# Six late output stores moved to another queue, and a score-operand load requested earlier

## The chip, the cores and the metric

The kernel runs on one core of a Trainium2 chip. The metric is the device time of one execution in microseconds (us). A core has five engines that run their own instruction streams and meet only at semaphores: TensorE (PE; its weight loads are listed as PEld), VectorE (DVE), ScalarE (ACT), GpSimd (POOL) and SyncE (SP). In this kernel SP does nothing but issue DMA transfers; POOL computes and also issues some. In the profile a name such as SPq or POOLq is the queue of that engine, where it waits and issues.

## The reference

One input `x` (2048 rows of 576, float32) is normalised; an attention block of 32 heads of 18 columns and a bilinear feed-forward block are both computed from it, and joined:

```
xn = layernorm(x)
s  = (softmax(q k^T * 18**-0.5) v, heads joined) @ wo      # q, k, v = xn @ wqkv
g  = silu(((xn @ w_gate) * (xn @ w_up)) @ w_down)          # inner width 4608
out = x + s * g
```

## The kernel before

Products on TensorE are made from pairs of a high and a low part of each number, so that several narrow matrix products add up to a precise one. The kernel has three stages.

**The opening** (to about 200 us) normalises `x`, makes q, k and v and puts them into DRAM scratch.

**The middle** (to about 2530 us) runs attention and the feed-forward block at once on TensorE. Attention takes the heads h = 0 to 31 in turn. For each head there are two passes over 64 scores (16 row blocks by 4 column blocks): the first pass ("a", L585) makes scores only to take row maxima on DVE (L587), the second ("b", L617) makes the transposed scores, which ACT exponentiates (L619). Then come the products with v (L628). The feed-forward block takes 72 units (4 chunks of 512 rows, 18 groups of 256 inner columns) with gate and up products (L667) and down products (L709).

The score passes read two kinds of stacked operands in SBUF. `pairs` are two tiles that alternate between heads; `ring` is a single tile that all heads use in turn, in two halves of 1024 columns each. `load_ring(r, h, k)` fills half k for head h, in rows 0 on (r = 0, for pass a) or rows 64 on (r = 64, for pass b), with three DMAs on SP's queue (L242). The first half serves the scores 0 to 31 of a pass, the second half 32 to 63. A load may go out when the head before has done its last score with that half.

The order of all this is not written out by hand: `order()` simulates the engines with fixed durations (`clk`, `free`, `banks`, `queue`) and emits instructions as its clock advances. A load that has become possible is put into a list `stacks` by `feed` (called before each score). It leaves the list in one of two ways: at the end of a gate block, where up to two of the listed loads are sent, or at a fixed score of the pass, by the table at L947, if it is still waiting then. `send` issues it and books its bytes on the simulated DMA queue; scores are held until their operands have arrived by that booking.

SP executes its queue strictly in order. Between the ring loads stand loads of gate and up weights (`wgu`, L182, 1152 KB, which wait until TensorE has finished with the buffer), of down weights (`wd`, L217), of the swapped halves of the feed-forward activations (`hx`, L699), of `xc` (L361, L364) and of `vt` (L573).

**The end** (from about 2530 us) multiplies the attention result with `wo`, tile by tile: 16 tiles t of 128 rows, each in two halves of 288 columns (L1218). `give(t, ps, last)` finishes a tile. For each half DVE multiplies the product in PSUM by the gate (L1227); then `x` is added and the tile stored. With `last` false, POOL adds (L1232) and the whole tile of 288 KB is stored by a DMA that POOL issues (L1234). With `last` true, DVE adds (L1229) and each half of 144 KB is stored by SP (L1230). Before the change only tile 15 has `last` true. After `give(t)` the kernel fetches what tile t + 6 needs (`xi`, `gin`; L831, L833), on SP's queue, so that the last fetch stands behind `give(9)`. POOL also does the last step of the gates of tiles 12 to 15 here (L765). L1283 is the end of the program, where every engine drains and all meet.

Of the kernel before, what the change touches and what calls it, by code (L numbers as in the profile page):

```python
# [40 lines left out]
def kernel(  # L41
# [10 lines left out]
    nc = tc.nc  # L52
# [5 lines left out]
    NT = S // 128  # L58
# [31 lines left out]
    out2 = out.rearrange("o s d -> (o s) d")  # L90
# [43 lines left out]
    def chore(all=True):  # L134
        q = (all and chores) or later
        if q:
            f, a = q.pop(0)
            f(*a)
# [5 lines left out]
    def ready(done, key):  # L144
        while key not in done:
            assert chores or later
            chore()
# [419 lines left out]
    with ExitStack() as mid:  # L567
# [240 lines left out]
        def high(k, c):  # L808
            if k == 0:
                hi[c] = fin["ep"].tile([128, 5, 512], FR, name="hi", bufs=2)  # L810
            nc.scalar.activation(hi[c][:, k, :], lo[k][:, 512 * c:512 * c + 512].bitcast(FT), AF.Copy)

        def low(k, c):
            part = lo[k][:, 512 * c:512 * c + 512]
            if k < 4:
                nc.vector.tensor_tensor(part, part.bitcast(FT), hi[c][:, k, :].bitcast(FT), op=OP.subtract)
            else:
                nc.vector.tensor_tensor(hi[c][64:128, 4, :], part[64:128].bitcast(FT), hi[c][64:128, 4, :].bitcast(FT),
                                        op=OP.subtract)
# [6 lines left out]
        def fetch(t):  # L826
            rows = slice(t * 128, (t + 1) * 128)
            if t < 12:
                ready(sdone, t)
                gin[t] = fin["ep"].tile([128, D], FT, name="gin", bufs=7)  # L830
                nc.sync.dma_start(gin[t], sg[rows, :])  # L831
            xi[t] = fin["ep"].tile([128, D], FT, name="xi", bufs=8)
            nc.sync.dma_start(xi[t], x2[rows, :])  # L833
# [94 lines left out]
        def send(want, now):  # L928
            f, a = want
            f(*a)  # L930
            arrives[f.__name__, *a] = moved(now, 0.44 if f is load_pair else 0.22)
# [6 lines left out]
        def feed(r, h, i):  # L938

            if i == 0:  # L940
                if h:
                    stacks.append((load_ring, (r, h, 1)))
                if h + 1 < H and (r or h):
                    stacks.append((load_pair, (r, h + 1)))
            if i == 32 and h + 1 < H:
                stacks.append((load_ring, (r, h + 1, 0)))
            for at, want in ((20, (load_ring, (r, h, 1))), (48, (load_pair, (r, h + 1))), (52, (load_ring, (r, h + 1, 0)))):  # L947
                if i == at and want in stacks:
                    stacks.remove(want)
                    send(want, max(clk))  # L950

        def a_next(r=0):
            nonlocal na
            h, i = divmod(na, N)
            feed(0, h, i)
            a_item(h, i, r)
            slot = turn["a"] % 2
            turn["a"] += 1
            banks["a"][slot] = engine("DVE", issue(r, LONG), 0.60) + EARLY
            na += 1  # L960
            if i == N - 1:
                max_fold(h)
                max_rows(h)
                rows_done[h] = engine("DVE", 0.0, 0.85) + ROWS
# [5 lines left out]
        def b_next(r=1):  # L970
            nonlocal nb
            h, i = divmod(nb, N)
            feed(64, h, i)
            if i == 16 and h % 2 == 0 and h // 2 + 1 < H // 2:
                load_v(h // 2 + 1)
            b_item(h, i, r)
            slot = turn["b"] % 2
            turn["b"] += 1
            end = engine("ACT", issue(r, LONG), 0.495)
            banks["b"][slot] = end + EARLY  # L980
            nb += 1
            if i % 4 == 3:
                due.append((h, i // 4, end + 0.03))
# [222 lines left out]
    def banks_of(t):  # L1206
        return [bank("ab"[t % 4], 2) if t % 4 < 2 else bank("g", 1, 2 * (t % 4) - 4 + h) for h in range(2)]
# [5 lines left out]
    def product(t, h, p, ps):  # L1213
        a, e = p
        c, r = divmod(t, 4)
        w = wov["w"][:, a, :] if a < 8 else wov["w2"][:, a - 8, :]
        o = lo[e - 4][:, t * 128:(t + 1) * 128] if 4 <= e < 8 else hi[c][:, min(e, 4), r * 128:(r + 1) * 128]
        nc.tensor.matmul(ps[h][:, 0:HALF], o, w[:, h * HALF:(h + 1) * HALF], start=p == ALL[0], stop=p == ALL[-1])  # L1218

    def give(t, ps, last=False):  # L1220
        y = ys[:, t % 4, :]
        ready(sdone, t)
        g = gin.pop(t)
        xt = xi.pop(t)
        for h in range(2):
            cs = slice(h * HALF, (h + 1) * HALF)
            nc.vector.tensor_tensor(y[:, cs], ps[h][:, 0:HALF], g[:, cs], op=OP.mult)  # L1227
            if last:
                nc.vector.tensor_tensor(y[:, cs], y[:, cs], xt[:, cs], op=OP.add)  # L1229
                nc.sync.dma_start(out2[t * 128:(t + 1) * 128, cs], y[:, cs])  # L1230
            else:
                nc.gpsimd.tensor_tensor(y[:, cs], y[:, cs], xt[:, cs], op=OP.add)  # L1232
        if not last:
            nc.gpsimd.dma_start(out2[t * 128:(t + 1) * 128, :], y)  # L1234

    ys = wpool.tile([128, 4, D], FT, name="ys", tag="wd", bufs=1)
    ps = {t: banks_of(t) for t in range(4)}
# [6 lines left out]
    for t in range(NT):  # L1244
        if t >= 4:
            ps[t] = banks_of(t)
        for h in range(2):
            for p in ORDER[2] if t < 4 else ALL:
                product(t, h, p, ps[t])
        for _ in range((2, 0, 0, 0, 2, 2, 1, 0, 2, 2, 1, 0, 0, 0, 0, 0)[t]):  # L1250
            if split:
                k, c = split.pop(0)
                high(k, c)
                low(k, c)
        give(t, ps.pop(t), t == NT - 1)
        if t + 6 < NT and t + 6 not in xi:
            fetch(t + 6)
        for _ in range((1, 1, 3, 3)[t % 4] if t < 12 else 4):
            chore()
# [28 lines left out]
```

## Time and profile before

| | us |
|---|---|
| median of 3 runs (2599.17 to 2603.44) | 2601.77 |
| the profiled execution, whole | 2602.83 |
| its span, first to last instruction | 2601.1 |
| TensorE busy in the span | 2576.5 |
| VectorE busy | 1919.9 |
| ScalarE busy | 1462.6 |
| GpSimd busy | 590.7 |

The granted clock of TensorE was 0.998 of full speed. "Busy" counts computing instructions; time in which a queue waits, drains or issues a DMA is listed apart. A row of the waits has the engine that waited, the line and tile, the releaser, and then us in total, times, and the longest. A row of a timeline has start, duration, engine, line, operation, output and inputs, and the count of merged instructions; in brackets stands the idle time before it with what ended it. A row for one source line has count, shortest, median and longest duration in ns, and the first and last start in us.

### The profile page before, as it was taken

How to read it: one execution, taken by the hardware profiler on the slowest of the kernel's cores; microseconds unless marked ns; L12 is line 12 of the kernel's file. 1: busy time of each engine (PE TensorE's matmuls, PEld its weight loads, DVE VectorE, ACT ScalarE, POOL GpSimd, SP SyncE). 2: the span in 40 equal slices, each digit the busy share in tenths (PEclk: the TensorE clock that was granted, in tenths of full speed). 3: DMA queues.
4: the chain of work that ended last, by engine and by line, in shares of the span. 5: the costliest groups of instructions: out<-in, count | busy, mean ns of one | idle time of the engine just before them, and what ended most of it. 6: DMA issues, size and time to landing. Idle time of an engine off the chain costs nothing.

```text
span 2601.1 us, 59086 instructions
## 1 busy us (share of the span) xinstructions
PE 2576.5 (99%) x24360; PEld 2109.3 (81%) x24360; DVE 1919.9 (74%) x3373; ACT 1462.6 (56%) x2698; POOL 590.7 (23%) x658
## 2 busy tenths in 40 slices
PE   8999999999999999999999999999999999999998
PEld 6899877788878788878878878877788888877878
DVE  6208777777768888877788788777788888777537
ACT  5222666666655555655555565555555665555561
POOL 3114444434421111111111112111111211111115
PEclk9999999999999999999999999999999999999999
DMA  7799989888786666565676556656686666665566
GB/s 237 221 283 275 269 226 227 227 217 220 218 190 181 178 180 178 171 182 157 177 195 176 167 172 181 177 164 174 157 202 157 175 184 175 176 174 168 150 187 232
DMA packets 195433, 504.57 MB, mean 194 GB/s; under 512 B 58096, under 2 KB 116080, under 8 KB 156124
## 3 DMA queue, kind: packets, MB, share of 16 engines
q1 hardware_dynamic: 184812, 487.58, 67.1%
q0 software_dynamic: 10352, 13.22, 1.9%
q8 instruction: 192, 3.15, 0.5%
q14 instruction: 77, 0.63, 0.1%
HBM read 312.21 MB, written 107.61 MB: 161 GB/s over the span
## 4 chain that ended last, share of the span: by engine, by line
PE 97%; DVE 1%; DMA 1%; ACT 0%; SPq 0%; issue 0%; ACTq 0%; DVEq 0%
PE pg L667 34%; PE pg L628 17%; PE pg L709 16%; PE pa L585 11%; PE pb L617 9%; PE pg L395 2%; PE pa L341 2%; PE pb L341 2%; PE pg L1218 1%; PE pa L1218 1%; PE pb L1218 1%; DMA ring<-sqk 0%; DMA hx<-hs 0%; ACT xn L289 0%; DMA xin<-in_A_x_dram 0%
## 5 line engine op out<-in xcount | busy, mean ns | idle before, releaser
L587 DVE TENSOR_REDUCE mx<-pa 128x1 f32<-128x512 f32 x2048 | 1361.8, 684 | 159.7 <-PE pa L585 73.3
L619 ACT ACTIVATE pt<-pb 128x512 f32<-128x512 f32 x2048 | 1155.1, 597 | 566.8 <-PE pb L617 484.4
L667 PE MATMUL pg<-xc,wgu 64*128 64x512 f32 x7776 | 1397.5, 392 | 0.3 <-DMA xc<-sx 0.3
L667 PEld LDWEIGHTS pg<-xc,wgu 64*128 64x128 f32 x7776 | 1056.3, 186 | 49.8 <-DMA xc<-sx 0.7
L617 PE MATMUL pb<-pair,ring 56*128 56x512 f32 x2006 | 789.1, 399 | 2.2 <-DMA ring<-sqk 2.2
L585 PE MATMUL pa<-pair,ring 54*128 54x512 f32 x2001 | 784.7, 398 | 0.3 <-DVE mx L587 0.3
L709 PE MATMUL pg<-wd,hs 64*128 64x288 f32 x3408 | 536.6, 292 | 1.2 <-DVE acc L737 1.2
L709 PE MATMUL pg<-wd,hx 64*128 64x288 f32 x3408 | 528.6, 292 | 0.4 <-DMA hx<-hs 0.4
L709 PEld LDWEIGHTS pg<-wd,hs 64*128 64x128 f32 x3408 | 473.4, 186 | 5.8 <-DVE acc L737 1.9
L709 PEld LDWEIGHTS pg<-wd,hx 64*128 64x128 f32 x3408 | 467.8, 185 | 4.4 <-DMA hx<-hs 1.0
L628 PE MATMUL pg<-pt,vt 128*32 128x512 f32 x4096 | 456.5, 596 | 0.0
L683 POOL TENSOR_TENSOR hs<-us,hs 128x512 fp32r<-128x512 f32 x144 | 186.2, 1293 | 1129.5 <-ACT hs L682 1112.9
L585 PEld LDWEIGHTS pa<-pair,ring 54*128 54x128 f32 x2001 | 363.2, 184 | 81.7 <-issue 47.8
L617 PEld LDWEIGHTS pb<-pair,ring 56*128 56x128 f32 x2006 | 364.7, 184 | 14.4 <-issue 3.4
L628 PEld LDWEIGHTS pg<-pt,vt 128*32 128x32 f32 x4096 | 125.9, 110 | 285.8 <-issue 281.9
L634 DVE TENSOR_TENSOR oc<-oc,pg 128x512 f32<-128x512 f32 x69 | 47.4, 687 | 323.5 <-PE pg L628 323.3
L737 DVE TENSOR_TENSOR acc<-acc,pg 128x288 f32<-128x288 f32 x544 | 234.0, 443 | 27.0 <-PE pg L709 24.2
L682 ACT ACTIVATE hs<-us 128x512 fp32r<-128x512 f32 x144 | 91.0, 632 | 154.2 <-DVE us L679 151.6
L648 POOL DMA_DIRECT2D sot<-oc x124 | 64.1, 523 | 332.8 <-DVE oc L645 330.7
L607 POOL DMA_DIRECT2D pair<-mt x128 | 78.0, 615 | 226.0 <-DVE mt L602 223.8
L632 ACT ACTIVATE oc<-pg 128x512 f32<-128x512 f32 x32 | 19.2, 599 | 189.3 <-PE pg L628 189.3
L191 POOL TENSOR_TENSOR wgu<-wraw,wgu 128x384 fp32r<-128x384 f32 x108 | 108.4, 1017 | 75.3 <-ACT wgu L190 70.4
(128 smaller groups left out, 1384.0 us busy)
## 6 DMA issues: line engine op xcount, KB each, us to landing
wgu<-swg SPq DMA_DIRECT2D x102, 1152.0 KB
hx<-hs SPq DMA_DIRECT2D x142, 512.0 KB
wd<-swd SPq DMA_DIRECT2D x50, 1152.0 KB
swg<-wgu SPq DMA_DIRECT2D x36, 1152.0 KB
pair<-sqk SPq DMA_DIRECT2D x192, 144.0 KB
ring<-sqk SPq DMA_DIRECT2D x384, 72.0 KB
swd<-wd SPq DMA_DIRECT2D x18, 1152.0 KB
sqk<-hl SPq DMA_DIRECT2D x32, 512.0 KB
```

The lines of the kernel that those rows point to most:

```text
L191: nc.gpsimd.tensor_tensor(w[:, 9 + b:12 + b, :], raw[:, b:b + 3, :], w[:, b:b + 3, :].bitcast(FT), op=OP.subtract)
L341: nc.tensor.matmul(p, wq[b, a], xcs[c][:, e, :], start=n == 0, stop=n == len(PAIRS) - 1)
L585: nc.tensor.matmul(p, q[rows, t * 128:(t + 1) * 128], k[rows, c * 512:(c + 1) * 512], start=True, stop=True)
L587: nc.vector.tensor_reduce(mx[h][:, t, c:c + 1], p, axis=AX.X, op=OP.max)
L617: nc.tensor.matmul(p, k[rows, t * 128:(t + 1) * 128], q[rows, c * 512:(c + 1) * 512], start=True, stop=True)
L619: nc.scalar.activation(pt[t, c], p, AF.Exp, scale=scale)
L628: nc.tensor.matmul(p[32 * c:32 * c + 32, :], vt[h // 2][:, t, 6 * (h % 2):6 * (h % 2) + 32], pt[t, c], start=t == ts[0], stop=t == ts[-1])
L667: nc.tensor.matmul(ps, gw[n][half[r], a, :], xg[i][half[r], e, :], start=k == 0, stop=k == len(TERMS) - 1)
L682: nc.scalar.activation(hj[:, 0, :], h32, AF.Copy)
L683: nc.gpsimd.tensor_tensor(hj[:, 1, :], h32, hj[:, 0, :].bitcast(FT), op=OP.subtract)
L709: nc.tensor.matmul(ps[:, 0:HALF], (hx if k else hs)[u][half[r], j, a, s * 128:(s + 1) * 128], dw[u][half[r], k, j, e, :], start=n == 0, st ...
L737: nc.vector.tensor_tensor(a, a, ps[:, 0:HALF], op=OP.add)
```

## The change

Three places. The second half of the ring, if it is still waiting in `stacks`, is sent at score 10 of its own pass instead of score 20. Tiles 10 to 15 are stored through SP's queue instead of POOL's (tiles 10 to 13 as whole tiles at L1234; tile 15 was on SP's already). And tile 14 is treated like tile 15: DVE adds `x`, and the two halves are stored apart.

```
-            for at, want in ((20, (load_ring, (r, h, 1))), (48, (load_pair, (r, h + 1))), (52, (load_ring, (r, h + 1, 0)))):
+            for at, want in ((10, (load_ring, (r, h, 1))), (48, (load_pair, (r, h + 1))), (52, (load_ring, (r, h + 1, 0)))):
                 if i == at and want in stacks:
                     stacks.remove(want)
                     send(want, max(clk))
...
         if not last:
-            nc.gpsimd.dma_start(out2[t * 128:(t + 1) * 128, :], y)
+            (nc.gpsimd if t < 10 else nc.sync).dma_start(out2[t * 128:(t + 1) * 128, :], y)
...
-        give(t, ps.pop(t), t == NT - 1)
+        give(t, ps.pop(t), t >= 14)
```

What this does to the instruction streams: TensorE's and ScalarE's rows stand in the same order as before. Three pieces of the other streams follow; a row has the line, the operation, output and inputs, and the first output's shape, with a count where equal rows follow each other.

POOL, the end of the program (`ys` is the output tile, `gl` a gate, `out_dram` the output):

```order
 L1234 DMA out_dram<-ys 128x576
 L1232 TENSOR_TENSOR ys<-ys,xi 128x288 x2
-L1234 DMA out_dram<-ys 128x576
 L765 TENSOR_TENSOR gl<-gl,acc_11507 128x576
-L1232 TENSOR_TENSOR ys<-ys,xi 128x288 x2
-L1234 DMA out_dram<-ys 128x576
-L1232 TENSOR_TENSOR ys<-ys,xi 128x288 x2
-L1234 DMA out_dram<-ys 128x576
+L1232 TENSOR_TENSOR ys<-ys,xi 128x288 x4
 L765 TENSOR_TENSOR gl<-gl,acc_11507 128x576
 L1232 TENSOR_TENSOR ys<-ys,xi 128x288 x2
```

POOL issues no DMA after tile 9's, and its last instruction is the addition of tile 13. Behind this piece the old stream has three more rows, the store of tile 13 and the addition and store of tile 14; the new one has none.

SP, the end of the program:

```order
 L831 DMA gin<-sg 128x576
 L833 DMA xi<-in_A_x_dram 128x576 x5
-L1230 DMA out_dram<-ys 128x288 x2
+L1234 DMA out_dram<-ys 128x576 x4
+L1230 DMA out_dram<-ys 128x288 x4
 L1283 UNCONDITIONAL_BRANCH
```

The stores of tiles 10 to 13 and of the halves of tiles 14 and 15 stand behind every load of the kernel.

SP, at the change from the first to the second chunk of the feed-forward block (`ring` rows are `load_ring`, three DMAs each):

```order
 L364 DMA xc<-sx 64x1024 x5
 L699 DMA hx<-hs 64x2048 x2
-L242 DMA ring<-sqk 18x1024 x3
-L182 DMA wgu<-swg 128x2304
-L242 DMA ring<-sqk 18x1024 x3
-L182 DMA wgu<-swg 128x2304
+L242 DMA ring<-sqk 18x1024 x6
+L182 DMA wgu<-swg 128x2304 x2
 L242 DMA pair_1148<-sqk 18x2048 x3
 L242 DMA ring<-sqk 18x1024 x3
```

The second of the two ring loads stands ahead of the weight load that it stood behind. Over the whole program 22 ring loads move like this: 18 ahead of a `wgu` load, two ahead of a `wd` and an `hx` load, one ahead of two steps of the `xc` loads, and one ahead of `vt` and a store and refill of raw weights. No other load changes its place among the rest.

## The prediction

> **What bounds the kernel now.** I read the page's busy times and its chain first, then who TensorE waited for, then the last 15 us.
>
> ```profile
> PE 2576.5 (99%) x24360; PEld 2109.3 (81%) x24360; DVE 1919.9 (74%) x3373; ACT 1462.6 (56%) x2698; POOL 590.7 (23%) x658
> PE 97%; DVE 1%; DMA 1%; ACT 0%; SPq 0%; issue 0%; ACTq 0%; DVEq 0%
> ```
>
> The first row is the busy time of each engine, the second the chain that ended last, by engine. TensorE sets the time nearly everywhere. Its instruction order is not changed, so a gain must come from a stall of TensorE that goes, or from outside its work. The waits of TensorE's queue say how much there is of the first kind:
>
> ```profile
> PE pb L617 <- DMA ring<-sqk: 2.2, 1, 2.2
> PE pg L709 <- DMA hx<-hs: 0.4, 1, 0.4
> PE pg L667 <- DMA xc<-sx: 0.3, 1, 0.3
> ```
>
> TensorE waited for a ring load once, 2.2 us, and for all DMAs together 2.9 us. Earlier ring loads cannot bring more than that. The rest must come from the end. The end of the program, L1283, queue by queue:
>
> ```profile
> L1283 SPq EVENT_SEMAPHORE  x12: 17/28/1191, 2593.2 to 2601.0; - x12
> L1283 POOLq EVENT_SEMAPHORE  x4: 17/17/17, 2600.3 to 2600.9; - x4
> L1283 POOLq DRAIN  x3: 40/102/8418, 2591.9 to 2600.8; - x3
> L1283 SPq DRAIN  x3: 7/7/7, 2595.1 to 2600.5; - x3
> ```
>
> SP has seen all stores land at 2595.1, where its first drain stands. POOL's first drain begins at 2591.9 and takes 8.418 us: 2591.9 + 8.4 = 2600.3, where POOL's first semaphore step follows. Only then do the engines meet, and 0.8 us later the span is over (2601.1). So POOL's drain ends last, and SP waits for it 2600.3 - 2595.1 = 5.2 us. Is it data that POOL still waits for?
>
> ```profile
> 2593.00:2595.00 2.00, 0.00 (x0) 0.00 (x0) 0.00 (x0) 0.00 (x0) 0.00 (x0) 0.58 0.72 264
> 2595.00:2600.00 5.00, 0.00 (x0) 0.00 (x0) 0.00 (x0) 0.00 (x0) 0.00 (x0) 0.50 0.00 0
> ```
>
> These are two windows; the last two columns are the DMA engines' busy share and GB/s. After 2595.0 nothing moves and no engine computes. The drain outlasts the data by 5 us. What stands just ahead of it is a DMA that POOL issued:
>
> ```profile
> L1234 POOL DMA_DIRECT2D out_dram<-ys x15: 557/559/583, 2547.4 to 2591.9; - x15
> L1230 SPq DMA_DIRECT2D out_dram<-ys x2: 344/344/344, 2591.9 to 2592.8; - x2
> 2574.97 0.56 POOL L1234 DMA_DIRECT2D out_dram<-ys  x1 [0.30 <-POOL ys L1232]
> ```
>
> POOL's fifteenth and last store starts at 2591.9, with the drain. The other two drains of POOL (0.10 and 0.04 us) follow within half a microsecond of the long one, with nothing issued between, so a drain as such is cheap; the long one carries something from the DMAs before it. The third row is tile 9's store, the tenth, which becomes POOL's last: 2575.0.
>
> **The change, part by part.** *The stores of tiles 10 to 14 leave POOL.* If the drain lasts until 8.4 us after POOL's last DMA issue, it now lasts until 2575.0 + 8.4 = 2583.4. POOL still adds then, so nothing of it is left, and the end is set by SP's last store. When does that go out? DVE and POOL at the end:
>
> ```profile
> 2586.00 0.76 DVE L1227 TENSOR_TENSOR ys<-pb,gl 128x288 f32<-128x288 f32 x2
> 2586.67 0.45 DVE L1227 TENSOR_TENSOR ys<-pg,gl 128x288 f32<-128x288 f32 x1
> 2587.51 0.46 DVE L1227 TENSOR_TENSOR ys<-pg,gl 128x288 f32<-128x288 f32 x1 [0.39 <-PE pg L1218]
> 2589.43 0.46 DVE L1227 TENSOR_TENSOR ys<-pg,gl 128x288 f32<-128x288 f32 x1 [1.46 <-PE pg L1218]
> 2589.92 1.99 DVE L1229 TENSOR_TENSOR ys<-ys,xi 128x288 f32<-128x288 f32 x1
> 2591.84 0.44 DVE L1227 TENSOR_TENSOR ys<-pg,gl 128x288 f32<-128x288 f32 x1
> 2592.31 0.46 DVE L1229 TENSOR_TENSOR ys<-ys,xi 128x288 f32<-128x288 f32 x1
> 2586.18 1.42 POOL L765 TENSOR_TENSOR gl<-gl,acc 128x576 f32<-128x576 f32 x1 [0.73 <-DVE gl L762]
> 2587.56 1.57 POOL L1232 TENSOR_TENSOR ys<-ys,xi 128x288 f32<-128x288 f32 x2
> 2590.03 1.56 POOL L1232 TENSOR_TENSOR ys<-ys,xi 128x288 f32<-128x288 f32 x2
> 2590.76 0.42 PE L1218 MATMUL pg<-wos,hi 128*128 128x288 f32 x2
> ```
>
> The same addition on DVE took 0.46 us alone and 1.99 us beside POOL's additions of tile 14 (1.56 us from 2590.03, 0.46 + 1.56 = 2.02): DVE stood still while POOL worked, and POOL's pair was not longer than the pair before it (1.57). So two additions more on DVE are not simply 0.92 us. *Tile 14's first addition* follows the product of 2586.67, at 2587.1, when POOL is in L765 and then in tile 13's additions, until 2587.56 + 1.57 = 2589.1. I let it wait until then. From 2589.1 DVE has seven instructions (addition, product, addition of tile 14, then product, addition, product, addition of tile 15) of 0.47 us from start to start (2591.84 to 2592.31): 2589.1 + 3.3 = 2592.4. Their inputs are there: TensorE ends at 2591.2, and the product that needs it starts at 2591.4. Before, the last addition ended at 2592.8. So these two additions cost nothing; they even end the interference with tile 15, since POOL is empty by then. Cover gone, they would cost what DVE lost in the row above: 1.5 us for one of tile 15's additions.
>
> The Trainium skill's page "SBUF — State Buffer", section "Who interferes with whom", says that a DVE instruction with two SBUF inputs and a GpSimd instruction that reads SBUF exclude each other for a whole instruction. It speaks against putting additions on DVE; the trace agrees (1.99 against 0.46 us). Without that rule tile 14's first addition would go through at once, DVE would end at 2592.2, bound by TensorE, and the sum below would be 0.2 us better.
>
> *The last store.* It was issued at 2592.8, and SP was through at 2595.1: 2.3 us. From 2592.4 this gives 2594.7, and with the 0.8 us of the meeting 2595.5. Against the span of 2601.1 the gain is 5.6 us. Bounds: with one addition of tile 15 still held for 1.5 us the end is 2597.0, a gain of 4.1. The other way, the 2.3 us were taken beside POOL's store of 288 KB; at the 264 GB/s of the window these are 1.1 us, and without them and the 0.2 us above the end is 2594.2, a gain of 6.9. I take 5.6, since both waits are dated by rows and the last store is alone by then.
>
> *SP's side.* Six stores more than before, at 0.34 us each. Is a load behind them?
>
> ```profile
> 2566.65 0.33 SPq L833 DMA_DIRECT2D xi<-in_A_x_dram  x1
> 2591.94 1.20 SPq L1230 DMA_DIRECT2D out_dram<-ys  x2
> ```
>
> SP's last load is issued at 2566.65 and it idles until 2591.94; tile 10's addition ends after 2575. The stores delay nothing. POOL loses 0.56 us of issue and 0.30 us of waiting a tile, but its additions wait for DVE, so this hides as well.
>
> *The ring loads.* Is the one late ring load moved? The chain around that stall and SP's queue:
>
> ```profile
> 752.74 12.96 DMA ring<-sqk
> 765.84 0.40 PE pb L617
> 750.53 2.52 SPq L242 DMA_DIRECT2D ring<-sqk  x3
> 758.35 0.35 SPq L182 DMA_DIRECT2D wgu<-swg  x1
> 758.74 1.42 SPq L242 DMA_DIRECT2D ring<-sqk  x3
> ```
>
> The late load is the one issued at 750.53, behind the `xc` and `hx` loads. In the changed order it stands where it stood; what moves is the group of 758.74, which goes ahead of the `wgu`. So the 2.2 us stay. No other ring load was late, hence a second half that comes sooner saves nothing. Does it cost? It is issued into an idle SP: between 753.1 and 758.35 SP only waited for the `wgu` buffer. The last move is like it:
>
> ```profile
> 2461.12 2.21 SPq L699 DMA_DIRECT2D hx<-hs  x2
> 2473.47 0.33 SPq L182 DMA_DIRECT2D wgu<-swg  x1
> 2473.84 1.06 SPq L242 DMA_DIRECT2D ring<-sqk  x3
> ```
>
> SP is free from 2463.3 to 2473.47, and the 1.06 us of the ring group fit in. Bounds for all 22 moves: 2.9 us gained if every DMA stall went, and 22 x 1.06 = 23.3 us lost if each stood in the open. I take 0, near the first end, since the rows show SP waiting where the groups go.
>
> **The sum** is 5.6 us: 2602.83 - 5.6 = 2597.2 for the profiled execution, which lies 1.1 us above the median. From the median 2601.77 it is **2596.2 us**. A measurement of this kernel tells about 0.2% (5.2 us) from no change, and the forecast lies just beyond.
>
> **Rivals.** *The drain is paid when POOL ends, however old its last DMA.* Then it starts at 2589.1 and ends at 2597.5, the span ends at 2598.3, and the gain is 2.8: 2599.0. For it: there is one long drain in the trace, so nothing shows from what it counts. Against it: the two short ones. The page "DMA: Bandwidth & Descriptors" of the Trainium skill, section "Issuing engines are not separate DMA queues", says that choosing another issuing engine saves only the sequencer's time to start a transfer. By it the move would save issue time alone and leave the drain in place, which is this rival; no run here shows yet which of the two holds.
>
> *The ring stall goes too.* The `wgu` of 758.35 leaves later and no longer presses on the ring load that landed at 765.7. Then 2.2 us more: 2594.0. Against it: the moved ring group takes its place in the queue at once.
>
> *Slower: the moved ring loads hold up the loads behind them.* SP is in order; a group that waits for the last score of the head before, or only for its 1.06 us, delays `wgu` or `hx` and TensorE with it. It decides from the sixth exposed group (5.6 / 1.06); with all 22 exposed it is 2596.2 + 23.3 = 2619.5, with eleven 2607.9. Against it are the idle stretches above and that TensorE never waited for `wgu`; for it, `hx` was already 0.4 us late once.
>
> **Chances.** The forecast 0.74 (of it 0.61 beyond 0.2%, 0.13 within), the late drain 0.11, the ring stall gone 0.09, slower 0.06. So faster 0.61 + 0.09 = 0.70, same 0.13 + 0.11 = 0.24, slower 0.06. The forecast's own range is 2601.77 - 6.9 = 2594.9 to 2597.7. The range takes in both other faster cases and a part of the scatter of the runs (2599.17 to 2603.44): 2593.4 to 2599.3; left out are the slower case and the scatter beyond.
>
> **What would show it.** Right: POOL's first drain short, SP's first drain the last event at about 2594.7, the last DVE addition near 2592.4 and tile 14's first stretched to about 2.4 us; the wait for `ring` still 2.2 us. Wrong: a drain of 8.4 us from 2589 on (the first rival); a ring wait of zero; new rows of TensorE waiting for `wgu` or `hx`; or a DVE addition of tile 15 that is still 2 us long.

## The result, and the profile after

| | median us | lowest to highest | ratio to before, 95% interval |
|---|---|---|---|
| before (20 runs beside it) | 2601.45 | 2599.06 to 2604.0 | |
| changed (20 runs) | 2595.91 | 2592.58 to 2600.47 | 0.9978, 0.9972 to 0.9985 |

The change is faster by 0.22%, with an interval of 0.15 to 0.28%. The forecast was 2596.2 us. The profiled execution of the changed kernel took 2595.93 us, with a span of 2594.1 (before: 2602.83 and 2601.1). I read its profile in the order of the one before: busy times and chain, TensorE's waits, the end.

The page of the changed kernel, engines and chain:

```profile
PE 2575.6 (99%) x24360; PEld 2111.6 (81%) x24360; DVE 1919.0 (74%) x3375; ACT 1461.6 (56%) x2698; POOL 586.3 (23%) x651
PE 97%; DMA 1%; DVE 1%; SPq 0%; issue 0%; ACT 0%; POOL 0%; POOLq 0%
```

Its waits of TensorE for DMAs:

```profile
PE pb L617 <- DMA ring<-sqk: 0.9, 1, 0.9
PE pg L709 <- DMA hx<-hs: 0.7, 1, 0.7
```

TensorE's work is the same (2575.6 us against 2576.5), and its stalls for DMAs are 1.6 us instead of 2.9. The wait for the ring load has fallen from 2.2 us to 0.9. The end of the program, L1283, by queue:

```profile
L1283 POOLq EVENT_SEMAPHORE  x4: 17/17/17, 2593.3 to 2594.0; - x4
L1283 POOLq DRAIN  x3: 40/102/9528, 2583.5 to 2593.8; - x3
L1283 SPq DRAIN  x3: 7/7/7, 2593.2 to 2593.5; - x3
```

Here is the surprise. POOL's first drain is not short. It begins at 2583.5 and takes 9.528 us, to 2593.0. That is just ahead of SP's first drain at 2593.2, so SP now sets the end, as forecast, but the drain has not gone: it has slipped in front of SP by 0.2 us. What POOL did last, in its timeline:

```profile
2572.84 0.56 POOL L1234 DMA_DIRECT2D out_dram<-ys  x1 [0.30 <-POOL ys L1232]
2577.28 3.40 POOL L1232 TENSOR_TENSOR ys<-ys,xi 128x288 f32<-128x288 f32 x4
2582.58 1.44 POOL L765 TENSOR_TENSOR gl<-gl,acc 128x576 f32<-128x576 f32 x1 [1.89 <-DVE gl L762]
2583.97 1.58 POOL L1232 TENSOR_TENSOR ys<-ys,xi 128x288 f32<-128x288 f32 x2
```

POOL's last DMA is tile 9's store, at 2572.84. Its last addition ends at 2583.97 + 1.58 = 2585.55, and the drain ends 7.5 us after that, 20.2 us after the last DMA issue. Before, POOL's last instruction was a DMA issue; the drain ended 8.4 us after its start and 7.8 us after its end (2591.9 + 0.56). Both kernels fit a drain that is over about 7.5 to 7.8 us after the end of whatever POOL does last. VectorE's last instructions and SP's last stores:

```profile
2576.40 1.24 DVE L758 TENSOR_SCALAR gl<-gl 128x576 f32<-128x576 f32 x1
2585.29 0.58 DVE L1229 TENSOR_TENSOR ys<-ys,xi 128x288 f32<-128x288 f32 x1
2590.81 0.46 DVE L1229 TENSOR_TENSOR ys<-ys,xi 128x288 f32<-128x288 f32 x1
```

```profile
L1230 SPq DMA_DIRECT2D out_dram<-ys x4: 332/358/551, 2586.0 to 2591.3; - x4
```

No addition of DVE is stretched by POOL to more than 0.58 us, and DVE ends at 2591.27. The last store goes out at 2591.3 and SP has seen it land 1.9 us later.

**Where the span's 7.0 us came from.** TensorE's last products stand at the same place in both kernels, so the span splits there:

```profile
2589.86 0.42 PE L1218 MATMUL pg<-wos,hi 128*128 128x288 f32 x2
```

They end at 2590.28 (before 2590.76 + 0.42 = 2591.18). Behind them the span went on for 9.9 us before and for 3.8 us now: 6.1 us of the 7.0 are the end of the program. The other 0.9 us are the balance of two places that the windows show, the first two rows from the kernel before, the last two from the changed one (PE, PEld, DVE, ACT and POOL with counts, then the granted clock, DMA share and GB/s):

```profile
767.20:770.60 3.40, 3.40 (x24) 0.86 (x20) 0.00 (x0) 0.00 (x0) 0.00 (x0) 0.50 0.21 53
28.50:31.90 3.40, 3.40 (x17) 2.79 (x16) 1.93 (x4) 0.60 (x1) 1.23 (x3) 1.00 0.98 261
```

```profile
767.20:770.60 3.40, 3.40 (x36) 1.01 (x38) 0.00 (x0) 0.59 (x1) 0.00 (x0) 1.00 0.50 197
28.50:31.90 3.40, 3.40 (x11) 2.82 (x12) 2.35 (x4) 0.94 (x2) 1.63 (x3) 0.51 0.98 251
```

Each execution has one stretch of 3.4 us at half clock, in different places: before, just behind the 2.2 us ring stall; now in the opening, where the change moves nothing. Between them the middle gained 2.9 us (1.2 of stall and, as the last section shows, 1.7 of clock); since 0.9 is left, the opening gave back some 2.0 (the first transposed score, L617, starts at 262.3 before and at 264.3 now). That need not fall so in every execution.

### The profile page after: what moved, and what is told of

Read it like the earlier page. It is cut to its first block, busy times and chain, and to the rows that moved or that the text cites. A ratio compares the mean times of both kernels' runs of the same rounds, so it can differ in the third digit from the quotient of the medians.

```text
span 2594.1 us, 59094 instructions
## 1 busy us (share of the span) xinstructions
PE 2575.6 (99%) x24360; PEld 2111.6 (81%) x24360; DVE 1919.0 (74%) x3375; ACT 1461.6 (56%) x2698; POOL 586.3 (23%) x651
## 4 chain that ended last, share of the span: by engine, by line
PE 97%; DMA 1%; DVE 1%; SPq 0%; issue 0%; ACT 0%; POOL 0%; POOLq 0%
PE pg L667 35%; PE pg L628 17%; PE pg L709 16%; PE pa L585 11%; PE pb L617 9%; PE pg L395 2%; PE pa L341 2%; PE pb L341 2%; PE pg L1218 1%; PE pa L1218 1%; PE pb L1218 1%; DMA hx<-hs 0%; DMA ring<-sqk 0%; DMA wraw<-in_A_wqkv_dram 0%; DMA wvraw<-in_A_wqkv_dram 0%
## 5 line engine op out<-in xcount | busy, mean ns | idle before, releaser
L617 PE MATMUL pb<-pair,ring 56*128 56x512 f32 x2006 | 789.0, 399 | 0.9 <-DMA ring<-sqk 0.9
L617 PEld LDWEIGHTS pb<-pair,ring 56*128 56x128 f32 x2006 | 364.7, 185 | 12.2 <-ACT us L672 1.3
L634 DVE TENSOR_TENSOR oc<-oc,pg 128x512 f32<-128x512 f32 x69 | 47.5, 688 | 320.0 <-PE pg L628 319.8
```

The source lines that it names most:

```text
L617: nc.tensor.matmul(p, k[rows, t * 128:(t + 1) * 128], q[rows, c * 512:(c + 1) * 512], start=True, stop=True)
```

## The experiments

Two theories were on trial for the end. **A**, the prediction's: the drain counts from POOL's last DMA, so a drain whose DMA is old is over. **B**: it counts from POOL's last instruction, however old its DMAs are. All diffs are against the changed kernel. For all runs the end of the program is told from the end of TensorE's last product, which takes out the scatter of what comes before (each row is one profiled execution):

| us after TensorE's last product | POOL's last DMA issue | POOL's last instruction ends | POOL's drain ends | SP's first drain | span ends |
|---|---|---|---|---|---|
| before | 0.7 | 1.25 | 9.09 | 3.90 | 9.87 |
| changed | -17.4 | -4.73 | 2.72 | 2.96 | 3.79 |
| end alone (table at 20) | -16.0 | -3.35 | 4.10 | 2.96 | 4.99 |
| ring alone | 0.1 | 0.67 | 8.51 | 3.32 | 9.29 |
| tile 14 as before | -17.7 | -2.33 | 5.12 | 3.02 | 5.91 |
| stores 10 to 13 on POOL | -1.0 | -0.40 | 7.36 | 3.20 | 8.14 |
| no DMA on POOL at all | none | -3.73 | -3.66 | 3.11 | 3.87 |
| one addition of tile 15 on POOL | -14.3 | -0.43 | 7.02 | 2.95 | 7.91 |
| one ring load | -16.6 | -4.24 | 3.21 | 2.96 | 4.10 |
| tile 13 too, and a second ring load | -15.7 | -4.88 | 2.57 | 2.91 | 3.75 |

**1. The end alone.** The ring table is set back:

```
-            for at, want in ((10, (load_ring, (r, h, 1))), ...
+            for at, want in ((20, (load_ring, (r, h, 1))), ...
```

> The six stores and tile 14 on VectorE as in the change, the ring table back at score 20. From TensorE's last product to the end of the span the kernel before took 9.9 us and the changed one 3.8. If the gain is all at the end (the prediction), this kernel has 3.8 there too, the ring wait is back at about 2.2 us, and it gains 5.6 to 6.1 us (ratio 0.9977 to 0.9979). If the earlier ring loads carry a part, it gains 1 to 3 us less than the changed kernel (ratio 0.9985 to 0.9990).

Measured: 2596.69 us, 0.9981 (0.9973 to 0.9990). The changed end alone carries the gain, within the intervals. In this execution the span ended 5.0 us after TensorE and not the expected 3.8: POOL ended 1.4 us later against TensorE than in the changed kernel's, and its drain (4.10) ended behind SP (2.96), so the drain still set the end. The 1.4 us stand in the traces long before the stores: ACT waited longer for a load of the attention result (`o`), first the changed kernel, then this run:

```profile
2540.28 0.63 ACT L811 ACTIVATE hi<-o 128x512 fp32r<-128x512 f32 x1 [4.07 <-DMA o<-sot]
```

```profile
2540.22 0.63 ACT L811 ACTIVATE hi<-o 128x512 fp32r<-128x512 f32 x1 [5.58 <-DMA o<-sot]
```

DVE waits for this step of ACT, and then makes its first product of the end (L1227): at 2542.78 in the changed kernel, 47.5 us ahead of TensorE's end, and at 2542.70 here, 46.0 ahead. In the ten profiled executions this lead lies between 45.8 and 47.7 us, in no order that follows the edits. With it the end of one and the same sequence came out at 3.8 us (changed kernel), 4.1 (experiment 7) and 5.0 (here). Why the load lands at different moments was not followed further.

**2. The ring loads alone.** The two edits of the end are set back:

```
-            (nc.gpsimd if t < 10 else nc.sync).dma_start(out2[t * 128:(t + 1) * 128, :], y)
+            nc.gpsimd.dma_start(out2[t * 128:(t + 1) * 128, :], y)
...
-        give(t, ps.pop(t), t >= 14)
+        give(t, ps.pop(t), t == NT - 1)
```

> The ring table at score 10, the end as before: 9.9 us from TensorE's last product to the end of the span in any case. The prediction: the ring wait stays 2.2 us, ratio 1.000. The rival (the weight load that now leaves later no longer presses on the late ring load): the wait falls to about 0.9 us as in the changed kernel, and with the slowed clock behind it gone up to 2.9 us are gained (ratio 0.9989 to 0.9995).

Measured: 2600.41 us, 0.9996 (0.9987 to 1.0005): no change that can be told. The stall moved, by the waits of this run:

```profile
PE pg L667 <- DMA xc<-sx: 1.6, 3, 0.7
PE pg L709 <- DMA hx<-hs: 0.8, 1, 0.8
```

There is no wait for the ring here; instead 1.6 us are spent on `xc`. So all DMA stalls together are 2.4 us, against 2.9 before.

**3. Tile 14 as before**, added on POOL and stored whole, but on SP (table at 20, as in 4, 5 and 6):

```
-        give(t, ps.pop(t), t >= 14)
+        give(t, ps.pop(t), t == NT - 1)
```

> Stores of tiles 10 to 15 on SP, but tile 14's additions on POOL again (ring at score 20). POOL's last DMA is as old as in the changed kernel; POOL's last instruction is about 2.3 us later. Theory A of the prediction (the drain counts from POOL's last DMA): drain over before SP is through, 3.8 us from TensorE's end to the end, gain 5.6 or more. Theory B (the drain takes 7.5 to 7.8 us from the end of POOL's last instruction, whatever it is): POOL ends about 2.4 us before TensorE, its drain about 5.2 us after TensorE, 6.0 us to the end of the span, gain about 3.9.

Measured: 2597.12 us, 0.9985 (0.9976 to 0.9994); the span ended 5.9 us after TensorE. POOL's last DMA was as old as in the changed kernel, and the drain still moved with POOL's last addition: against A, for B. POOL's last addition and its drains:

```profile
2585.85 0.81 POOL L1232 TENSOR_TENSOR ys<-ys,xi 128x288 f32<-128x288 f32 x1 [0.83 <-DVE ys L1227]
L1283 POOLq DRAIN  x3: 40/102/8292, 2585.8 to 2594.6; - x3
```

The addition ends at 2586.66, and the drain at 2594.1, 7.4 us later.

**4. Tiles 10 to 13 stored by POOL**, tile 14 on DVE and SP:

```
-            (nc.gpsimd if t < 10 else nc.sync).dma_start(out2[t * 128:(t + 1) * 128, :], y)
+            nc.gpsimd.dma_start(out2[t * 128:(t + 1) * 128, :], y)
```

> Tiles 14 and 15 on VectorE, the stores of tiles 10 to 13 back on POOL (ring at score 20). POOL's last instruction is tile 13's store, started about 4.4 us before TensorE's end. Theory A: drain until 8.4 us after that start, 4.0 us after TensorE's end. Theory B: 7.5 us after its end, 3.7 us after TensorE's end. Both: about 4.6 us from TensorE's end to the end of the span, gain about 5.2; then the moved stores by themselves are worth less than 1 us, and tile 14's move carries the gain.

Measured: 2600.0 us, 0.9994 (0.9985 to 1.0003), the span's end at 8.1. The expectation missed, because it had POOL end sooner. The drain itself is B's again (7.8 us from the end of the last issue). POOL's and DVE's timeline, the last row from the kernel before:

```profile
2575.06 1.44 POOL L765 TENSOR_TENSOR gl<-gl,acc 128x576 f32<-128x576 f32 x1
2576.45 1.56 POOL L1232 TENSOR_TENSOR ys<-ys,xi 128x288 f32<-128x288 f32 x2
2579.83 1.56 POOL L1232 TENSOR_TENSOR ys<-ys,xi 128x288 f32<-128x288 f32 x2 [0.94 <-DVE ys L1227]
2586.67 0.58 POOL L1234 DMA_DIRECT2D out_dram<-ys  x1 [0.30 <-POOL ys L1232]
2575.35 2.99 DVE L758 TENSOR_SCALAR gl<-gl 128x576 f32<-128x576 f32 x1
2578.55 2.99 DVE L758 TENSOR_SCALAR gl<-gl 128x576 f32<-128x576 f32 x1
```

With its stores POOL is later; its gate step and a pair of additions then fall on DVE's L758, which takes 2.99 us as it did before, against 1.24 in the changed kernel; DVE's products come later, and POOL's next additions wait for them. So a store on POOL cost here not just its 0.56 us of issue but also what it pushed together.

**5. No DMA on POOL in the whole program.** All of POOL's transfers go to SP:

```
-                    nc.gpsimd.dma_start(rows, mt[32 * g:32 * g + 32, :])
+                    nc.sync.dma_start(rows, mt[32 * g:32 * g + 32, :])
...
-                    store(c, nc.gpsimd)
+                    store(c, nc.sync)
...
-                nc.gpsimd.dma_start(sg[t * 128:(t + 1) * 128, :], e)
+                nc.sync.dma_start(sg[t * 128:(t + 1) * 128, :], e)
...
-            (nc.gpsimd if t < 10 else nc.sync).dma_start(out2[t * 128:(t + 1) * 128, :], y)
+            nc.sync.dma_start(out2[t * 128:(t + 1) * 128, :], y)
```

> Every DMA that POOL issued in the whole program goes to SP's queue (pair and ring rows, attention output, gate store, all output stores); ring at score 20, tiles 14 and 15 on VectorE. The output stores now stand between SP's loads, so the whole time says little; the question is POOL's drain. In five kernels so far it ended 7.45 us after POOL's last computing instruction or 7.8 us after the end of its last DMA issue. If the 7.45 us belong to an engine that has issued DMAs, the drain is now under 0.2 us after POOL's last instruction. If they belong to POOL as such, it is 7.45 us again.

POOL's last additions in its timeline, and its drains at L1283:

```profile
2587.25 1.80 POOL L1232 TENSOR_TENSOR ys<-ys,xi 128x288 f32<-128x288 f32 x2
```

```profile
L1283 POOLq DRAIN  x3: 40/77/2611, 2586.5 to 2596.4; - x3
```

The drain takes 2.611 us from 2586.5, to 2589.1, and POOL's last addition ends at 2589.05. It is over at once. So of the ten kernels only the nine in which POOL issued DMAs have the 7.5 us, whether the last one was fresh or 20 us old. The single time was 2598.5 us, with the end at 3.9, no better than the changed kernel's 3.8, since SP's last store sets it in both. TensorE waited 2.1 us for `hx`, 1.8 for the ring and 1.3 for `wgu`; the ring wait is like that of the other kernels with the table at 20, and that the other two come from the transfers added to SP's queue is argued.

**6. POOL last, long after its last DMA.** One addition of tile 15 goes to POOL:

```
-                nc.vector.tensor_tensor(y[:, cs], y[:, cs], xt[:, cs], op=OP.add)
+                (nc.gpsimd if (t, h) == (15, 0) else nc.vector).tensor_tensor(y[:, cs], y[:, cs], xt[:, cs], op=OP.add)
```

> As the change's end (ring at score 20), but POOL adds the first half of tile 15. No DMA of POOL is younger than tile 9's. Theory A (drain counts from POOL's last DMA): 3.8 us from TensorE's end to the end of the span. Theory B (7.45 us from the end of POOL's last instruction): POOL ends about 0.45 us before TensorE, the drain 7.0 us after it, 7.8 us to the end of the span.

This tells A from B most sharply. POOL's timeline, from its last DMA and at its last instruction, and its drains at L1283:

```profile
2576.13 0.56 POOL L1234 DMA_DIRECT2D out_dram<-ys  x1 [0.30 <-POOL ys L1232]
...
2589.17 0.81 POOL L1229 TENSOR_TENSOR ys<-ys,xi 128x288 f32<-128x288 f32 x1 [0.22 <-DVE ys L1227]
```

```profile
L1283 POOLq DRAIN  x3: 40/102/8292, 2589.1 to 2597.9; - x3
```

The last addition ends at 2589.98 and the drain at 2589.1 + 8.3 = 2597.4, 7.4 us later and 21.3 us after the last DMA issue. The span ended 7.9 us after TensorE's last product, as B had it, and the one time was 2600.09 us. Against the first experiment, from which it differs by this addition alone, the end is 2.9 us later: one addition on POOL, with no DMA behind it.

**7. One ring load.** Of the 22 loads only the one beside the late load is moved, head 8's second half in pass a:

```
-            for at, want in ((10, (load_ring, (r, h, 1))), ...
+            for at, want in ((10 if (r, h) == (0, 8) else 20, (load_ring, (r, h, 1))), ...
```

> The change's end, and of the 22 moved ring loads one alone: the second half for head 8, pass a, which goes ahead of the weight load that stood behind the late ring load of head 7. In four kernels with the table at 20 TensorE waited 1.5 to 2.2 us for the late load, in two with the table at 10 it waited 0 and 0.9. If this one move does it, 0 to 1.0 here; if the other 21 do, 1.5 to 2.2.

One run, 2595.02 us. TensorE's waits for the ring in this run, and in the first experiment, which moves no ring load:

```profile
PE pb L617 <- DMA ring<-sqk: 0.7, 1, 0.7
```

```profile
PE pb L617 <- DMA ring<-sqk: 1.6, 1, 1.6
```

In the six kernels with the table at 20 (before among them) this wait was 1.4 to 2.2 us; in the three that send head 8's load ahead of the `wgu`, and change nothing else there, it was 0, 0.7 and 0.9. What the load does there shows in SP's timeline and in the chain around the stall, both of the changed kernel:

```profile
753.00 6.43 SPq L242 DMA_DIRECT2D ring<-sqk  x6
762.12 0.35 SPq L182 DMA_DIRECT2D wgu<-swg  x1
```

```profile
755.63 10.92 DMA ring<-sqk
```

The `wgu` left at 762.12 instead of 758.35, and the late load was 10.9 us under way instead of 13.0. That this is because the `wgu` shares the DMA engines with it for a shorter time is argued from these rows; no run changed the `wgu` alone.

**8. Tile 13 on DVE too, and the late ring load itself sooner:**

```
-... (52, (load_ring, (r, h + 1, 0)))):
+... (36 if (r, h) == (64, 6) else 52, (load_ring, (r, h + 1, 0)))):
...
-        give(t, ps.pop(t), t >= 14)
+        give(t, ps.pop(t), t >= 13)
```

> The whole change, and two steps more: tile 13 is added on VectorE too, and the late ring load of head 7 is sent at score 36 instead of 52, ahead of the last xc step and of hx. By theory B POOL ends with the gate of tile 15, about 6.3 us before TensorE, its drain 1.2 us after TensorE, so that SP's last store (3.0 us after) ends the program in every run: 3.8 us from TensorE's end to the end. The ring wait is zero. 0.5 to 2 us faster than the changed kernel: 2594 to 2595.5, ratio 0.9972 to 0.9977. By theory A the end is the same 3.8 us and only the ring wait is gained.

Measured: 2597.96 us, 0.9984 (0.9975 to 0.9993), not better than the changed kernel. The end is as good as before it (3.75), since SP's store was already what came last. The ring wait is gone, but a transfer that stood ahead of it now comes late, as TensorE's waits and the window behind this wait show:

```profile
PE pg L667 <- DMA xc<-sx: 2.8, 1, 2.8
```

```profile
759.00:763.00 4.00, 3.91 (x20) 3.16 (x22) 2.30 (x4) 1.71 (x3) 0.56 (x1) 0.57 0.76 159
```

The granted clock is 0.57 there. In this execution the ring load that went ahead of the last `xc` step only moved the stall, and made it longer. No run is shown to beat the changed kernel; the one time of the seventh (2595.02) lies inside the changed kernel's own scatter.

## Why the prediction was right, and where it was wrong

*What bounds the kernel.* Right. The gain came from behind TensorE's last product (6.1 us of the profiled span), and TensorE's work did not move.

*The drain.* This step failed: "If the drain lasts until 8.4 us after POOL's last DMA issue, it now lasts until 2575.0 + 8.4 = 2583.4." It ended at 2593.0. The runs put the first rival's mechanism in its place: in the nine kernels where POOL issued DMAs, the drain is over 7.4 to 7.5 us after POOL's last computing instruction (7.7 to 7.9 us after the end of its last DMA issue, where that came last), with last DMAs issued 8 to 23 us before the drain's end. The argument from the two short drains was wrong: they come behind the long one, so they show only that it isn't paid twice.

*Why the number held all the same.* The rival took this mechanism with POOL's end where it stood before, less its own work: 2589.1, 2.1 us ahead of TensorE's end, and so gave 2599.0. POOL ended 4.7 us ahead of it. About half of these 2.6 us is the change's doing. Without the stores POOL runs ahead of the gate steps, DVE's L758 takes 1.24 us instead of 2.99, and POOL's later additions find their products earlier: counted from DVE's first product of the end, tile 13's additions were done after 44.2 us before, and after 42.8 in the changed kernel (42.6 in experiment 1). This is a second step of the prediction that failed: "POOL loses 0.56 us of issue and 0.30 us of waiting a tile, but its additions wait for DVE, so this hides as well" put POOL's relief at nothing. The other half is luck: the profiled execution had that first product 47.5 us ahead of TensorE's end, and the one before 46.2. Together they bring the drain's end to 0.2 us before SP's; in experiment 1, without the luck, it was 1.1 us behind. Two errors met: a drain that did not go, and a POOL that was quicker than either case allowed. The stores alone do not do it: moving them is worth 3.2 us of the end (experiment 4 against 1), tile 14 another 0.9 (3 against 1; 2.1 against the changed kernel's execution), each by the moment at which POOL stops. The times agree: by the ends in the table the first four experiments should gain 4.9, 0.6, 4.0 and 1.7 us, and their medians lie 4.5, 0.8, 4.1 and 1.2 us under the 2601.18 of the kernel before beside them.

*Tile 14's first addition* was to wait for POOL until 2589.1, some 2.4 us. It took 0.58 us, since POOL was through at 2585.55. DVE ended at 2591.27, 1.0 us after TensorE; forecast were 2592.4 and 1.2. *The last store* took 1.9 us to SP's drain instead of the 2.3 taken from the kernel before, so SP's part of the end was mis-sized by 0.5 us: 3.8 us from TensorE's end to the span's, where 4.3 had been forecast. That put the gain at the end at 6.1 us instead of 5.6, within its bounds of 4.1 to 6.9. That the six stores and the two additions on DVE cost nothing was right.

*The ring loads* were put at 0, with the 2.2 us stall left as it was. As a sum this held: alone they gave 0.9996 (0.9987 to 1.0005), and the end alone 0.9981 against 0.9978 for both. The statement on the stall did not: it fell to 0.9 us, so the second rival was right that it moves, at about half its price (that the later `wgu` did it stays argued), and in one run the stall was traded for one on `xc`. "The moved ring group takes its place in the queue at once" overlooked that the group is 216 KB and the `wgu` 1152 KB. The slower rival had no trace: TensorE waited for no `wgu`, and for `hx` 0.7 us.

## What to carry to other kernels

Where an engine that issues DMAs drains last, look at what it does last, and not only at what it transferred last: here every microsecond by which POOL stopped sooner was a microsecond of the span, until SP's last store took over. Take the last work off such an engine as well as its last DMAs, and stop when the next end is reached (in the changed kernel's trace SP's drain, 0.2 us behind); more, as in experiment 8, brings nothing. Where two mechanisms would explain one long row, look for what each would do to the work around it too: the right size came here from a wrong reason.

## What the runs showed of the hardware

POOL, whose DMAs the profile lists as a queue of their own (`software_dynamic`), had a first drain at the end that was over 7.4 to 7.9 us after its last instruction, in nine kernels; with no DMA of POOL in the program it was over after 0.07 us. What is done in that time the traces do not show, nor how old POOL's last DMA would have to be for the drain to be short: none of the nine is older than 23 us. The Trainium skill's page "DMA: Bandwidth & Descriptors", section "Issuing engines are not separate DMA queues", says that starting DMAs from several engines only saves the time to start them. Here four stores, of some 0.56 us of issue each, cost 3.2 us on POOL: beyond the issue itself, by the work that they pushed together, with the 7.5 us always behind it.

The 2.2 us stall before had a second price. The products behind it, at half clock and at full clock (before, then the changed kernel):

```profile
766.23 7.91 PE L628 MATMUL pg<-pt,vt 128*32 128x512 f32 x56
```

```profile
767.09 6.21 PE L628 MATMUL pg<-pt,vt 128*32 128x512 f32 x56
```

The same 56 products took 1.7 us longer. The half clock lasted 3.4 us, which is the window that the page "TensorE: Matmul & The Clock Gate" of the Trainium skill gives in "What's actually happening". The same page of the Trainium skill, section "Why this matters for your kernels", asks to keep idle gaps under about 3 us. Here shorter ones were followed by half clock: the 2.2 us stall, the 2.8 us in experiment 8, and 2.7 us in the changed kernel's opening:

```profile
28.41 1.04 PE L325 MATMUL pg<-ident,xn 128*128 128x128 f32 x4 [2.68 <-DVE xcx L329]
```

But the length of the gap does not decide alone. Stalls of 1.4 to 1.8 us at the place of the ring stall were not followed by half clock, nor was one of 2.1 us in experiment 5; in the opening of experiment 1, half clock came about 1 us behind a gap of 1.4 us, as it did behind one of 1.3 us in experiment 4. The first two rows are from experiment 5, the others from experiment 1:

```profile
280.13 0.40 PE L709 MATMUL pg<-wd,hx 64*128 64x288 f32 x1 [2.08 <-DMA hx<-hs]
280.00:284.00 4.00, 3.80 (x45) 3.46 (x47) 2.66 (x5) 2.08 (x4) 0.78 (x1) 1.00 0.98 341
```

```profile
12.92 5.73 PE L341 MATMUL pb<-xcx,wgu 128*128 128x512 f32 x14 [1.39 <-ACT xcx L328]
15.00:16.00 1.00, 1.00 (x4) 0.81 (x3) 0.97 (x2) 1.00 (x2) 0.35 (x1) 0.50 0.17 28
```

What decides it stays open.
